# Attention and gated MLP on one core: the load of the next pair's values moved forward in the loop, partial outputs stored from SyncE, small products limited to 24 a pair

## The chip, the core and the metric

One core of one Trainium2 chip runs the whole program. The metric is device microseconds of one execution; the time before is the median of 3 runs. Engines have the profile's names: PE multiplies, PEld loads its weights, DVE, ACT and POOL do elementwise work, and SP only issues DMAs. An engine's queue runs in order: an instruction that waits holds all that stand behind it on the same engine.

## What is computed

Block-causal attention over 8 batches and 8 heads (576 positions of 64), then a gated MLP over the 4608 tokens of 512 features:

```python
scores = scale * np.matmul(q, k.transpose(0, 1, 3, 2))
scores = np.where(block_i >= block_j, scores, -1000000000.0)
attn = softmax(scores)                      # over the keys
x = (attn @ v).transpose(0, 2, 1, 3).reshape(B * S, H * D)
out = (1 / (1 + np.exp(-(x @ w_gate))) * (x @ w_val)) @ w_out
```

## The kernel before, in words

Two heads of one batch make a **pair**; there are 32, numbered p = 0 to 31, and four of them are a batch. The first stage goes through the pairs. While a pair's scores, softmax and value products run, PE's gaps are filled with products of the first third of the MLP (`mlp1`) for the batch before. The second stage, from about 660 us on, does the rest of the MLP with dense products (L1253, L1338).

Up to p = 7 the probabilities are transposed on PE. From p = 8 on (`rest`) DVE transposes them into `ZV` in blocks of 32, and the value products are 32x64 tiles, done in two runs of 144 rows each: `z_run` at the step `half` of the pair, and again at the step `AV`, which opens the next pair. The lists `JOIN` (p = 8) and `REST` (p = 9 to 31) give the order of a pair's steps, each with a number of places at which MLP products are dealt out; a pair of `REST` has 36. In `REST` the steps are: `AV` of the pair before, `s` and `t` (scores), `sl`, the transposes, `ml`, `half`, `r` (reciprocal sums to `r_d` and broadcast back as `rb`), `k`, `FX` (the pair before is finished: POOL multiplies `xT` by `rb` at L739, ACT cuts `XH` at L741, SP stores `xT_d` at L746), `q`, `v`.

The loads are SP's. Steps `k` and `q` load keys and queries of pair p+3 (L316, eight DMAs), step `v` loads the values of pair p+1 (L283, eight DMAs of 144 KB in runs of 256 bytes). Values of odd and even pairs have a buffer each: `VR` for even p, a part of the tile `ZV` for odd p. So a row `bank<-ZV,VR` is of an even pair and `bank<-ZV` alone of an odd one. A value load may start when the second run of the pair two before, which read the same buffer, is done. `behind` pins each value load behind the last query load (or `rb`) on SP, so SP's order is: r_d, k, rb, k, q, values, xT_d, and again r_d.

Each batch's `mlp1` ends with four copies out of PSUM by ACT (L866, into `ost`, two buffers), each stored to `part_d` (L869) by ACT's own DMA queue. All hardware DMAs, of whatever engine, share eight completion semaphores in turn, so a DMA also waits until the one eight before it in the program has landed; for the store this can be a value load that SP has still to issue.

`filling(p)` puts small products of one column (`bank<-ident`) in front of the first value run, so that PE's count of issued instructions, modulo 256, stands in `WINDOW` there. Each is two rows on PE.

Of the kernel before, what the change touches and what calls it, by code (L numbers as in the profile page):

```python
# [21 lines left out]
NX = 256  # L22
AHEAD = 3
KEEP = (52, 40)
WINDOW = (140, 152)

CONV_DUE = ([(0, 5), (0, 10), (1, 10), (2, 10), *((p, 9) for p in range(3, 7))], [(6, 1), (7, 2), (7, 8), (8, 1)])

# [1 line left out]
         ("tr3", 1), ("r", 0), ("ld", 0))  # L30
ALONE = (("S3", 1), ("TR2", 1), ("warm", 0), ("k", 1), ("S2", 1), ("q", 1), ("m3", 0), ("m2", 0), ("TRt", 1), ("t", 1), ("TRl", 1), ("sl", 1), ("AV", 2),
         ("tr3", 1), ("r", 0), ("FX", 0), ("ld", 0))
REST = (("AV", 0), ("s", 0), ("t", 9), ("sl", 3), ("tr3", 2), ("trt", 3), ("ml", 0), ("tr2", 0), ("trl", 0), ("half", 3),
        ("r", 3), ("k", 4), ("FX", 3), ("q", 3), ("v", 3))
JOIN = (("s", 0), ("t", 9), ("AV", 8), ("sl", 3), ("tr3", 2), ("trt", 3), ("ml", 0), ("tr2", 0), ("trl", 0), ("half", 2),
        ("r", 2), ("k", 2), ("q", 3), ("v", 2))
TURN = (("s3", 1), ("TR2", 1), ("k", 0), ("s2", 1), ("TRt", 1), ("q", 0), ("t", 1), ("TRl", 1), ("sl", 1), ("AV", 1),
        ("tr3", 1), ("r", 0), ("tr2", 1), ("trl", 1), ("trt", 3))
N_FIRST = 7
# [3 lines left out]
FETCH, FETCH_AT = 256, 192  # L43
# [6 lines left out]
def attn_glu_kernel(ctx: ExitStack, tc: tile.TileContext, q, k, v, w_gate, w_val, w_out, out):  # L50
    nc = tc.nc
# [3 lines left out]
    P = 128  # L55
# [8 lines left out]
    part_d = dram.tile([NTOK, DM], F32, name="part_d")  # L64
# [155 lines left out]
    with ExitStack() as s2:  # L220
# [55 lines left out]
        def load(p, what, queue=nc.sync):  # L276
            b, hp = pairs[p]
            h0 = 2 * hp
            if what == "v" and p > N_FIRST:
                VR = VRs[(p + 1) % 2]  # L280
                for a in range(4):
                    for h in range(2):
                        dma = nc.sync.dma_start(out=VR[32 * a:32 * a + 32, h],  # L283
                                                in_=v[b, h0 + h].rearrange("(t p) d -> p t d", p=32))
                        behind(dma.ins, last["SPq"])
                        last["SPq"] = dma.ins
                loads["SP"] = dma.ins
                return
            if what == "v":
                VS = VSs[p % 3]  # L290
                for h in range(2):
                    bulk(nc.sync.dma_start(out=VS[:, 0:4, h * D:(h + 1) * D],
                                           in_=v[b, h0 + h, 0:4 * P, :].rearrange("(t p) d -> p t d", p=P)))
                dma = nc.sync.dma_start(out=VS[64:128, 4, :].rearrange("p (h d) -> p h d", h=2),
                                        in_=v[b, h0:h0 + 2, 4 * P:S, :].rearrange("h p d -> p h d"))
                bulk(dma)
                loads["SP"] = dma.ins
                return
            if p <= NP:

                i, src = (0, k) if what == "k" else (1, q)
                r = rqks[p % 2].rearrange("p i s -> p (i s)").rearrange("p (t c) -> p t c", c=P)
                for h in range(2):
                    bulk(queue.dma_start(out=r[:, 4 * i:4 * i + 4, h * D:(h + 1) * D],
                                         in_=src[b, h0 + h, 0:4 * P, :].rearrange("(t p) d -> p t d", p=P)))
                dma = queue.dma_start(out=r[64 * i:64 * i + 64, 8, :].rearrange("p (h d) -> p h d", h=2),
                                      in_=src[b, h0:h0 + 2, 4 * P:S, :].rearrange("h p d -> p h d"))
                bulk(dma)
                if queue is nc.sync:
                    mark("SP", dma)  # L310
                return

            r, src = (rqks[p % 2][:, 0], k) if what == "k" else (rqks[p % 2][:, 1], q)
            for h in range(2):
                for j in range(2):
                    dma = bulk(queue.dma_start(  # L316
                        out=r[64 * h + 32 * j:64 * h + 32 * j + 32].rearrange("p (t a) -> p t a", a=32),
                        in_=src[b, h0 + h, :, 32 * j:32 * j + 32].rearrange("(t p) a -> p t a", p=32)))
                    if p > N_FIRST + 3:
                        last["SPq"] = dma.ins  # L320
# [5 lines left out]
        def filling(p):  # L326

            x = (FETCH_AT - issued[0] - WAITS[0] - WAITS[1] * p // 4) % FETCH
            lo, hi = WINDOW
            return 0 if lo <= x <= hi else -(-((x - hi) % FETCH) // 4)  # L330

        def mark(engine, ins):
            last[engine] = ins.ins
# [530 lines left out]
        def out_done(b, t, ps):  # L864
            ost = mp.tile([P, DM], F32, name="t" if b == B and t > 1 else "ost", bufs=2)
            nc.scalar.mul(out=ost, in_=ps, mul=0.5)  # L866
            if b < B:
                r = b * S + t * P
                nc.scalar.dma_start(out=part_d[r:r + P, :], in_=ost)  # L869
            else:  # L870
                for j in range(2):
                    r = (2 * t + j) * S + NM
                    nc.gpsimd.dma_start(out=part_d[r:r + 64, :], in_=ost[64 * j:64 * j + 64, :])
# [293 lines left out]
        for p in range(n + 1):  # L1167
            early_work(p, 0)
            pr = prep(p + 1) if p + 1 < n else iter(())
            now = attend(p) if p < n else None  # L1170
            tick = 0
            steps = (ALONE if p < NP else FIRST if p < N_FIRST else TURN if p == N_FIRST else
                     JOIN if p == N_FIRST + 1 else REST)
            ticks = sum(places for _, places in steps)
            lined[0] = line if N_FIRST < p < n else no_line
            for what, places in steps:
                if what.startswith(("AV", "TR", "FX")):
                    if prev:
                        prev(what.lower() if what in ("AV", "FX") else what.lower()[:2] + what[2:])
                    if prev and what == "AV" and pairs[p - 1][1] == NP - 1:  # L1180
                        pb = pairs[p - 1][0]
                        mlp = itertools.chain(mlp, mlp1(pb, mbank if p < n else bank))
                        left += F1 * 6 * NC + 3 * F1 * 4
                elif what in "kq":
                    next(pr, None)
                    if p >= N_FIRST and p + 3 < n:
                        load(p + 3, what)
                elif what == "v":
                    if p + 1 < n:
                        load(p + 1, "v")  # L1190
                elif what == "ld":
                    for x in "kq":
                        load(p + 3, x)
                elif now:
                    hot[0] = p > N_FIRST and (hot[0] or what == "s")
                    now(what)
                    if what == "trt" and p > N_FIRST:
                        hot[0] = False
                        settle()
                new = what == "AV" and pairs[p - 1][1] == NP - 1  # L1200
                if p <= N_FIRST and new and p:
                    rate = (left - KEEP[0]) / (4 * TICKS)
                elif p > N_FIRST and (new or what == steps[0][0]):
                    i = p % NP
                    rate = max(0, left - KEEP[1]) / (ticks - tick + (NP - 1 - i) * PLACES) if i or new else 1.0
                for _ in range(places if now else 6 if what == "AV" else 0):
                    pe_ticks.append(pe_last[0])
                    acc += rate
                    while acc >= 1:
                        acc -= 1  # L1210
                        left -= 1
                        issued[0] += 2
                        ins = next(mlp, None)
                        if ins is not None:
                            if dealt and p > N_FIRST:
                                behind(ins, dealt[0])
                            dealt[:] = [ins]
                            recent[:] = [*recent[-7:], ins]
                            if hold:
                                behind(ins, hold[0])  # L1220
                            ahead_by = 0 if p > N_FIRST + 1 and what == "t" or p != N_FIRST + 1 and what == "trt" else AHEAD
                            if len(pe_ticks) > ahead_by:
                                behind(ins, pe_ticks[-1 - ahead_by])
                    tick += 1
                    convert_to(p, tick)
                    early_work(p, tick)
            run(pr)
            if p == N_FIRST:
                load(p + 1, "v")
            if 0 < p and p + 2 <= N_FIRST:  # L1230
                load(p + 2, "v")
            prev = now
# [267 lines left out]
```

## Time and profile before

| | |
|---|---|
| median of 3 runs (lowest to highest) | 1266.76 us (1261.48 to 1269.65) |
| the profiled execution, its span | 1266.42 us, 1264.6 us |
| mean granted TensorE clock | 0.957 |
| pairs 9 to 28 (153.2 to 581.0) | 427.8 us |
| PE busy in them | 379.1 us |

A pair is counted from its first `bank<-KH,QH` product of 512 columns to that of the next pair; pair 20 begins at 390.2, pair 21 at 414.2, pair 22 at 431.3. In the windows view each row is one stretch: its length, then busy time and number of instructions of each engine (PE, PEld, DVE, ACT, POOL), then the granted clock of PE as a share of full speed, the DMA engines' busy share and GB/s. In a timeline a row gives start, length, engine, line, operation and tiles, the number of merged instructions, and in brackets the idle time before it and what ended it. SPq and ACTq rows are the issuing of DMAs, not their transfer.

### The profile page before, as it was taken

What the parts mean: (1) busy time and instruction counts of PE and PEld (TensorE: products, weight loads), DVE (VectorE), ACT (ScalarE), POOL (GpSimd) and SP (SyncE); (2) the same over time, 40 slices, a digit from 0 to 9 for tenths busy, and PEclk for the clock granted to TensorE, in tenths of its full rate; (3) what the DMA queues carried; (4) which work ended last, traced back from release to release, by engine and by line L of the source; (5) the groups of instructions that cost most, each with busy time, mean ns of one, the idle gap of its engine ahead of it and who ended that gap; (6) DMA issues with size and microseconds to landing.
All of it is one profiled execution on the core that took longest, in us unless ns stands there. A gap on an engine that the chain in (4) does not pass through costs nothing.

```text
span 1264.6 us, 32228 instructions
## 1 busy us (share of the span) xinstructions
PE 1186.0 (94%) x12851; PEld 947.3 (75%) x12851; DVE 888.2 (70%) x1748; ACT 573.7 (45%) x1370; POOL 340.4 (27%) x381
## 2 busy tenths in 40 slices
PE   8898889899898997999989999999999999999998
PEld 5565667677677775777768888888888888888888
DVE  5877645566556754675798695888999976768565
ACT  5866345455444543553524344354454432323222
POOL 3445313232133231323330110111111234142402
PEclk9999889889888987898999999999999999999999
DMA  7656565858676768586854114265387956253522
GB/s 162 171 140 143 110 132 99 154 101 127 126 136 126 142 107 165 98 134 129 161 146 136 67 51 134 47 187 158 69 217 246 319 174 209 87 179 108 167 95 89
DMA packets 396486, 175.42 MB, mean 139 GB/s; under 512 B 323248, under 2 KB 363184, under 8 KB 395696
## 3 DMA queue, kind: packets, MB, share of 16 engines
q1 hardware_dynamic: 388992, 161.92, 54.7%
q10 hardware_dynamic: 6960, 10.39, 2.5%
q8 instruction: 101, 1.65, 0.6%
q0 software_dynamic: 384, 1.05, 0.2%
q14 instruction: 49, 0.40, 0.1%
HBM read 125.96 MB, written 47.33 MB: 137 GB/s over the span
## 4 chain that ended last, share of the span: by engine, by line
PE 65%; DMA 8%; SPq 5%; DVE 5%; issue 1%; ACT 1%; ACTq 0%; DVEq 0%
PE b L1253 25%; PE bank L354 11%; PE m L160 11%; PE b L1338 7%; PE m L1338 7%; PE m L167 4%; DMA ZV<-in_v_dram 3%; DMA VR<-in_v_dram 2%; SPq L316 2%; PE bank L160 1%; SPq L283 1%; PE bank L167 1%; DMA r_d<-rT 1%; DVE XL L1069 1%; DMA xT_d<-xT 1%
## 5 line engine op out<-in xcount | busy, mean ns | idle before, releaser
L1253 PE MATMUL b<-XH,w 128*128 128x512 f32 (+1 forms) x1120 | 320.8, 368 | 1.0 <-ACT p L1271 0.9
L1253 PEld LDWEIGHTS b<-XH,w 128*128 128x128 f32 x1120 | 203.5, 188 | 37.5 <-ACT p L1271 1.3
L1253 PE MATMUL b<-XL,w 128*128 128x512 f32 (+1 forms) x560 | 205.6, 368 | 0.0
L498 ACT ACTIVATE P<-bank,nm 128x512 f32<-128x512 f32 (+3 forms) x256 | 131.9, 525 | 21.3 <-DVE nm L490 20.8
L490 DVE TENSOR_REDUCE nm<-bank 128x2 f32<-128x1024 f32 (+3 forms) x128 | 100.6, 816 | 31.5 <-ACT bank L531 29.7
L1253 PEld LDWEIGHTS b<-XL,w 128*128 128x128 f32 x560 | 105.5, 188 | 17.6
L1066 ACT CAST XH<-XB 128x1024 fp32r<-128x1024 f32 (+1 forms) x72 | 66.9, 943 | 89.4 <-DVE XB L1064 54.5
L535 DVE MEMSET bank<- 64x128 f32 x24 | 4.0, 165 | 137.0 <-PE bank L354 137.0
L354 PE MATMUL bank<-ZV,VR 32*64 32x80 f32 (+4 forms) x3456 | 72.6, 275 | 25.4 <-DMA VR<-in_v_dram 22.8
L167 PE MATMUL m<-wo,hH 128*128 128x512 f32 x256 | 93.0, 434 | 2.6 <-ACT ost L866 2.6
L1338 PE MATMUL m<-wo,hH 128*128 128x512 f32 x288 | 93.3, 389 | 0.0
L1338 PE MATMUL b<-wo,hH 128*128 128x512 f32 x288 | 92.9, 389 | 0.0
L656 DVE STREAM_TRANSPOSE ZV<-P 128x512 f32<-128x512 f32 (+1 forms) x192 | 87.5, 491 | 7.0 <-ACT P L498 5.9
L1051 POOL TENSOR_TENSOR XB<-XB 128x256 f32<-128x256 f32 x30 | 24.6, 820 | 246.3 <-DMA XB<-xT_d 191.6
L354 PEld LDWEIGHTS bank<-ZV,VR 32*64 32x64 f32 x3456 | 60.4, 152 | 37.1 <-DMA VR<-in_v_dram 30.4
L1069 DVE TENSOR_TENSOR XL<-XB,XH 128x1024 fp32r<-128x1024 f32 (+1 forms) x72 | 78.2, 1091 | 13.6 <-ACT XH L1066 13.4
L160 PE MATMUL m<-XH,wg 128*128 128x512 f32 x240 | 86.7, 421 | 0.0
L160 PE MATMUL m<-XH,wv 128*128 128x512 f32 x240 | 84.7, 411 | 0.9 <-DVE h L205 0.9
L354 PE MATMUL bank<-ZV 32*64 32x48 f32 (+5 forms) x3680 | 77.5, 260 | 3.2 <-DMA ZV<-in_v_dram 3.0
L354 PEld LDWEIGHTS bank<-ZV 32*64 32x64 f32 (+1 forms) x3680 | 61.8, 132 | 18.7 <-issue 4.6
L739 POOL TENSOR_TENSOR xT<-xT,rb 128x576 f32<-128x576 f32 x24 | 34.6, 1440 | 131.9 <-ACT xT L714 83.7
L167 PEld LDWEIGHTS m<-wo,hH 128*128 128x128 f32 x256 | 53.1, 213 | 16.5 <-ACT ost L866 5.2
(214 smaller groups left out, 2493.7 us busy)
## 6 DMA issues: line engine op xcount, KB each, us to landing
VR<-in_v_dram SPq DMA_DIRECT2D x96, 144.0 KB
ZV<-in_v_dram SPq DMA_DIRECT2D x96, 144.0 KB
XB<-xT_d SPq DMA_DIRECT2D x48, 256.0 KB
prr<-part_d SPq DMA_DIRECT2D x46, 256.0 KB
part_d<-ost SPq DMA_DIRECT2D x36, 256.0 KB
part_d<-ost ACTq DMA_DIRECT2D x32, 256.0 KB
xT_d<-xT SPq DMA_DIRECT2D x28, 288.0 KB
rqk<-in_k_dram SPq DMA_DIRECT2D x108, 72.0 KB
```

The costliest lines, as they stand in the source:

```text
L160: mm = nc.tensor.matmul(ps, lhsT=lh, rhs=rh, start=(i == 0), stop=(i == n - 1))
L167: mm = nc.tensor.matmul(ps, lhsT=lh[:, f, t * P:(t + 1) * P], rhs=rh, start=(f == i == 0), stop=(f == F1 - 1 and i == 2))
L316: dma = bulk(queue.dma_start(out=r[64 * h + 32 * j:64 * h + 32 * j + 32].rearrange("p (t a) -> p t a", a=32), in_=src[b, h0 + h, :, 32 * j ...
L354: pe_last[:] = [nc.tensor.matmul(*args, **kw).ins]
L490: line("DVE", nc.vector.tensor_reduce(out=nm[:, c0:c0 + 2], in_=ps[:, :, c:c + P * (i + 1)], axis=AX.X, op=ALU.max, negate=True), rest)
L498: line("ACT", nc.scalar.activation(out=Pi[:, h], in_=ps[:, h, c:c + n], func=AF.Exp, bias=nm[:, c0 + h:c0 + h + 1], accum_out=sm[:, 5 * h ...
L656: line("DVE", nc.vector.transpose(out=dst[:, :, :4 * ZG].rearrange("p b (g x) -> p b g x", g=4)[:, :, :i + 1, :32], in_=Pi[:, h].rearrange ...
L739: nc.gpsimd.tensor_mul(out=xT, in0=xT, in1=rb)
L1066: cut = nc.scalar.copy(out=XO[j][0][:, a:b, c], in_=x)
L1069: sub = nc.vector.tensor_sub(out=XO[j][1][:, a:b, c], in0=x, in1=XO[j][0][:, a:b, c].bitcast(F32))
L1253: mm = nc.tensor.matmul(ps, lhsT=lh, rhs=rh, start=(first and k == 0), stop=(k == n - 1), skip_group_check=not first)
L1338: mm = nc.tensor.matmul(po[t], lhsT=lh[:, f, t * P:(t + 1) * P], rhs=rh, start=(half == 0 and i == 0), stop=(half == 1 and i == 5))
```

## The change

Three edits. The step `v` stands behind `t` in `REST` (9 places after the scores) and behind `AV` in `JOIN`; its places went to `q`, so no other step moves; for p = 7 the load of pair 8's values moves from the pair's end to behind `sl`. The 32 stores of `part_d` are issued by SP instead of ACT. `filling` gives at most 24.

```diff
-WINDOW = (140, 152)
+WINDOW, MOST = (140, 152), 24
-REST = (("AV", 0), ("s", 0), ("t", 9), ("sl", 3), ("tr3", 2), ("trt", 3), ("ml", 0), ("tr2", 0), ("trl", 0), ("half", 3),
-        ("r", 3), ("k", 4), ("FX", 3), ("q", 3), ("v", 3))
-JOIN = (("s", 0), ("t", 9), ("AV", 8), ("sl", 3), ("tr3", 2), ("trt", 3), ("ml", 0), ("tr2", 0), ("trl", 0), ("half", 2),
-        ("r", 2), ("k", 2), ("q", 3), ("v", 2))
+REST = (("AV", 0), ("s", 0), ("t", 9), ("v", 0), ("sl", 3), ("tr3", 2), ("trt", 3), ("ml", 0), ("tr2", 0), ("trl", 0), ("half", 3),
+        ("r", 3), ("k", 4), ("FX", 3), ("q", 6))
+JOIN = (("s", 0), ("t", 9), ("AV", 8), ("v", 0), ("sl", 3), ("tr3", 2), ("trt", 3), ("ml", 0), ("tr2", 0), ("trl", 0), ("half", 2),
+        ("r", 2), ("k", 2), ("q", 5))
-            return 0 if lo <= x <= hi else -(-((x - hi) % FETCH) // 4)
+            return 0 if lo <= x <= hi else min(-(-((x - hi) % FETCH) // 4), MOST)
-                nc.scalar.dma_start(out=part_d[r:r + P, :], in_=ost)
+                nc.sync.dma_start(out=part_d[r:r + P, :], in_=ost)
+                    if what == "sl" and p == N_FIRST:
+                        load(p + 1, "v")
-            if p == N_FIRST:
-                load(p + 1, "v")
```

What it moves on SP, between the query loads of pair 8's step `q` and the `rb` loads of pair 9. Before:

```order
L316 DMA rqk_93<-in_k_dram 32x18x32 x2
L316 DMA rqk_93<-in_q_dram 32x18x32 x4
L283 DMA ZV<-in_v_dram 32x18x64 x8
L746 DMA xT_d<-xT 128x576
L588 DMA r_d<-rT 9x32 x4
L316 DMA rqk_92<-in_k_dram 32x18x32 x2
L593 DMA rb<-r_d 64x512
```

The same place of the changed kernel:

```order
L316 DMA rqk_93<-in_k_dram 32x18x32 x2
L316 DMA rqk_93<-in_q_dram 32x18x32 x4
L869 DMA part_d<-ost 128x512
L283 DMA VR_95<-in_v_dram 32x18x64 x8
L746 DMA xT_d<-xT 128x576
L869 DMA part_d<-ost 128x512 x2
L588 DMA r_d<-rT 9x32 x4
L316 DMA rqk_92<-in_k_dram 32x18x32 x2
L593 DMA rb<-r_d 64x512
```

The value load keeps its place between q and xT_d, but it is now that of pair 10 (`VR`), where it was that of pair 9 (`ZV`): one pair earlier. Stores of `ost` stand before and behind it.

On ACT, in the pair in which a batch's first three copies to `ost` come (pair 12; pairs 16, 20 and so on are alike). Before:

```order
L869 DMA part_d<-ost 128x512 x2
L430 CAST KH<-KQ 128x576
L431 ACTIVATE QH<-KQ 128x448
L741 CAST XH_428<-xT 128x512
L866 ACTIVATE ost<-m 128x512
L869 DMA part_d<-ost 128x512
L714 COPY xT<-bank_2935 128x2x4x32
```

Now:

```order
L430 CAST KH<-KQ 128x576
L431 ACTIVATE QH<-KQ 128x448
L741 CAST XH_428<-xT 128x512
L866 ACTIVATE ost<-m 128x512
L714 COPY xT<-bank_2943 128x2x4x32
```

The stores are gone from in front of the copies to `xT` (L714), which free the PSUM banks that the next pair's scores need; nothing else on ACT moves. On PE only the small products change: 52, 16, 12 and 11 of them in pairs 8 to 11 become 24, 24, 24 and 19, and the 20 pairs after those keep their 14 or 15. DVE and POOL have the same order as before.

## Rows read from the trace of the kernel before

**Rows 1.** Page, busy time of the engines, share of the span, instructions.

```profile
PE 1186.0 (94%) x12851; PEld 947.3 (75%) x12851; DVE 888.2 (70%) x1748; ACT 573.7 (45%) x1370; POOL 340.4 (27%) x381
```

**Rows 2.** Windows: pairs 13, 19, 20, 22 and 23, and the sum of pairs 9 to 28.

```profile
241.40:265.40 24.00, 18.26 (x386) 14.48 (x384) 12.45 (x27) 9.82 (x30) 5.17 (x6) 0.86 0.64 120
...
373.80:390.20 16.40, 16.37 (x389) 13.17 (x384) 13.65 (x28) 9.89 (x30) 6.85 (x7) 1.00 0.61 109
390.20:414.20 24.00, 20.74 (x385) 16.01 (x382) 11.56 (x26) 9.82 (x30) 5.36 (x10) 0.86 0.76 151
...
431.30:455.10 23.80, 20.83 (x386) 16.25 (x382) 12.04 (x27) 10.09 (x30) 6.65 (x11) 0.86 0.79 136
455.10:471.30 16.20, 16.20 (x390) 13.06 (x382) 12.60 (x28) 9.83 (x30) 6.62 (x7) 1.00 0.65 100
...
sum 427.80, PE 379.06 PEld 298.66 DVE 247.52 ACT 199.19 POOL 120.84; mean PE 18.95 PEld 14.93 DVE 12.38 ACT 9.96 POOL 6.04
```

**Rows 3.** Windows: a stretch inside pair 20.

```profile
402.50:409.30 6.80, 6.18 (x140) 5.17 (x141) 0.97 (x2) 0.69 (x2) 2.98 (x6) 0.50 0.43 115
```

**Rows 4.** Waits of PE and ACT, whole run: us in total, times, longest.

```profile
PE bank L354 <- DMA VR<-in_v_dram: 22.8, 44, 1.2
PE bank L354 <- ACT xT L714: 22.7, 7, 5.7
...
ACT xT L714 <- DMA ZV<-in_v_dram: 26.4, 4, 8.2
```

**Rows 5.** Timeline of PE, pair 20, around its first value run.

```profile
398.11 0.43 PE L354 MATMUL bank<-ident 32*64 32x1 f32 x30
...
403.56 2.34 PE L354 MATMUL bank<-ZV,VR 32*64 32x48 f32 x130 [0.49 <-DMA VR<-in_v_dram]
```

**Rows 6.** Timeline of SP's queue: value loads and what follows them, four places.

```profile
287.22 6.16 SPq L283 DMA_DIRECT2D ZV<-in_v_dram  x8
293.48 1.87 SPq L746 DMA_DIRECT2D xT_d<-xT  x1
...
307.57 5.93 SPq L283 DMA_DIRECT2D VR<-in_v_dram  x8
...
393.62 5.96 SPq L283 DMA_DIRECT2D VR<-in_v_dram  x8
...
400.63 2.23 SPq L588 DMA_DIRECT2D r_d<-rT  x4
...
411.97 5.68 SPq L283 DMA_DIRECT2D ZV<-in_v_dram  x8
...
474.83 5.62 SPq L283 DMA_DIRECT2D VR<-in_v_dram  x8
...
494.17 6.05 SPq L283 DMA_DIRECT2D ZV<-in_v_dram  x8
...
520.32 5.62 SPq L283 DMA_DIRECT2D VR<-in_v_dram  x8
...
538.07 5.83 SPq L283 DMA_DIRECT2D ZV<-in_v_dram  x8
```

**Rows 7.** Timeline of ACT: a copy and its store (pairs 12, 13), and pair 20.

```profile
238.78 0.60 ACT L866 ACTIVATE ost<-m 128x512 f32<-128x512 f32 x1 [1.10 <-PE m L167]
247.13 0.33 ACTq L869 DMA_DIRECT2D part_d<-ost  x1
...
402.59 0.60 ACT L741 CAST XH<-xT 128x512 fp32r<-128x512 f32 x1
```

**Rows 8.** Timeline of POOL, pair 22: the product with rb.

```profile
434.31 1.44 POOL L739 TENSOR_TENSOR xT<-xT,rb 128x576 f32<-128x576 f32 x1 [2.32 <-DMA rb<-r_d]
```

**Rows 9.** Timeline of PE, pair 8, first value run.

```profile
144.57 1.40 PE L354 MATMUL bank<-ZV,VR 32*64 32x48 f32 x66 [1.83 <-issue]
```

**Rows 10.** Timeline of SP's queue behind the last pair.

```profile
659.02 2.08 SPq L961 DMA_DIRECT2D raw<-in_moe_w_gate_dram  x4
```

**Rows 11.** Instructions on the tensor part_d; SP's own stores of the second stage: ns min/median/max.

```profile
L1353 SPq DMA_DIRECT2D part_d<-ost x36: 320/411/1752, 766.0 to 995.9; - x36
```

## The prediction

> **What bounds the kernel now.** The page comes first. PE is busy 1186 of 1264.6 us [rows 1]; it sets the end, and a change counts only if it takes idle time or slow time from PE. The second stage has none to give, so I cut the first stage into pairs with the windows view. Pairs 9 to 28, all steady `REST` pairs, take 427.8 us, 21.4 each [rows 2]. But a pair that nothing disturbs takes 16.2 or 16.4 us with PE busy throughout at clock 1.00, and others take 24 at clock 0.86 [rows 2]. At 16.4 the twenty would take 328 us: some 100 us stand in the disturbed ones.
>
> The waits view says what disturbs them. PE waits 22.8 us in 44 pieces for `VR` and 22.7 us in seven for ACT's copy of `xT` [rows 4]. Each wait is paid twice: behind pair 20's broken value run the clock stands at 0.50 for 6.8 us [rows 3], which is 1.2 of 2.4 GHz.
>
> The timelines show how each arises. **Values late.** Pair 20's first value run is ready at 398.1, but its load is issued by SP from 393.62 for 5.96 us, and PE gets the last of it at 403.56 [rows 5, 6]: about 10 us from first issue to the last landing. SP could not be earlier, because the load stands behind r_d, k, rb, k and q. So there is a loop: the run of pair p+1 waits for its values, these for SP's lap, and the lap starts with r_d of pair p, whose sums come just when pair p's run does. It explains the alternation of 16 and 24: a pair that was stretched gives SP time, and the next finds its values there. **ACT held.** In pair 13 ACT has finished the copy to `ost` at 239.4, but its store goes out only at 247.13 [rows 7], while the copies of `xT` stand behind it; ACT's idle time there, up to 8.2 us and 26.4 in all, ends with a value load [rows 4], the one whose semaphore the store shares. This makes pair 13 24.0 us long.
>
> **The change, part by part.** *Values one pair earlier.* They keep SP's place behind q and before xT_d, so they still go out near the start of a pair; but they are needed in the middle of the next one, some 16 us later than now. 10 us of landing fit into that. The new wait is for the second run that last read the buffer; it ends where the pair begins, in pair 20 at 390.2, and SP comes to its load at 393.62 [rows 2, 6], so I cost it at nothing; an SP that came early would wait there, and r_d behind it too. The 22.8 us of waits and their slow stretches go, as far as SP keeps up.
>
> *Stores on SP.* ACT no longer stands before a store, so the 22.7 us go too. SP gets 32 more issues, on average one a pair. ACT issues one in 0.33 us, SP its own stores of the second stage in 0.41 median, 1.75 at most [rows 7, 11]. Where a store stands in front of r_d it partly fills time in which SP waits for the values to land anyway: I take 0.25 a pair, bounds 0 and 0.41.
>
> For this part a rule of the Trainium skill can be set against a row. ACT's store row lasts 0.33 us and starts 7.7 us after its copy ended [rows 7]. The page "DMA: Bandwidth & Descriptors", section "Issuing engines are not separate DMA queues", says that starting DMAs from several engines saves only the time the sequencer needs to initiate them, usually small. By it the move gives 32 x 0.33 = 10.6 us of ACT's time and leaves PE's wait on `xT`, 22.7 us: the sum below would come to 1231. The row contradicts this: what the store costs ACT is the wait in front of it. I go by the row.
>
> *What limits the pairs then.* With both waits gone PE could do a pair in 16.4 us, and SP's lap becomes the question. I read it from one value load to the next. Where r_d followed xT_d at once, a lap took 411.97 - 393.62 = 18.35 us, and 494.17 - 474.83 = 19.34; where SP rested a little before r_d, 538.07 - 520.32 = 17.75 [rows 6]. In none of these did SP wait long for PE. r_d right behind the values takes 2.23 us for its four issues [rows 6], because the values must land first. None of this changes, so SP is slower than PE: the next thing late is SP's `rb`, its stores, and at last the values again. I take 18.35 + 0.25 = 18.6 us a pair: 20 x 18.6 = 372.0, against 427.8 a gain of 55.8. Bounds: 17.75 with stores free (72.8), and 19.34 + 0.41 = 19.75 (32.8).
>
> *PE's lead.* PE may run ahead of SP until one of SP's products is missing. `rb` has about 8 us: POOL's product with it starts 3.0 us into pair 22 and takes 1.44 [rows 2, 8], and ACT's cut of its result comes 12.4 us into pair 20 [rows 2, 7]. A store of `ost` may have next to nothing, since the third copy of a batch reuses the first one's buffer. At the end, where no more keys and values are loaded, SP catches up, so the lead is kept: 4 us gained, bounds 0 and 8.
>
> *Small products.* 91 in pairs 8 to 11 before, 91 after: the same PE time. They move PE's place in its instruction stream, which the row of pair 8 prices: a value run broken for 1.83 us by "issue" [rows 9]. That stall can go (-1.8), or appear in pairs 8, 9 and 10 (+5.5 if all three are new). I take +1.
>
> *Stores behind the last pair.* There SP's weight loads leave in groups, one at 659.02 that takes 2.08 us [rows 10], and the third stores of batches 6 and 7 each stand behind such a group. ACT's copies have two buffers: I take +1, bounds 0 and 3.
>
> Sum against the profiled execution's own 1266.4 us (0.3 below the median of the runs): 1266.4 - 55.8 - 4 + 1 + 1 = 1208.6, so **1209 us**. With all bounds good 1266.4 - 72.8 - 8 - 1.8 = 1184, with all bad 1266.4 - 32.8 + 5.5 + 3 = 1242.
>
> **The rivals.** *PE sets the pace (0.10).* SP's laps could shrink when no run is late. Then 20 x 16.4 = 328: 1266.4 - 99.8 = 1167. Against it: no lap read here is under 17.75.
>
> *The stores cost SP what xT_d sometimes does (0.13).* xT_d behind the values took 1.87 us at 293.48, and that lap 307.57 - 287.22 = 20.35 [rows 6]; SP also rested in it, so it is a high price. Twenty such make 407: 1266.4 - 20.8 = 1246. A rule speaks for this: the Trainium skill, same page, "Queues, rings and completion order", says that on each DMA engine one queue's descriptors are taken in ring order while the engine takes turns between queues; a store from SP therefore stands behind the values' descriptors, where ACT's took turns with them. No run here shows such a store yet.
>
> *Nothing is gained (0.08).* If laps with stores take 21.4, or PE's waits only change their names, it stays at 1266, within 1% (1254 to 1279).
>
> *Slower (0.06).* The place is ACT's copy to `ost`: two buffers, a store that now stands behind eight value loads, and the copies of `xT` behind it on ACT. Each time it holds ACT as in pair 13, the pair costs 24.0 instead of 16.4. Two of a batch's four pairs hit give 20.2 a pair, still a gain; from three on the mean is 22.1, 0.7 over the 21.4 of now, and with four 24.0: 1281 to 1319, I say 1300. Against it: only the third copy of a batch follows its buffer's store closely.
>
> **The numbers.** The SP-paced case has 0.63 (1184 to 1242). About 1% is what a measurement of this kernel can tell from no change. Faster by more: 0.63 + 0.10 + 0.12 of the store case = 0.85; within 1%: 0.09; slower: 0.06. For 8 in 10 the range takes the SP-paced case, the store case up to 1250, and the near edge of the PE-paced one: 1172 to 1250.
>
> **What would show it.** Right: no PE wait on `VR` worth naming, none of ACT on a value load, SP issuing without rest from pair 9 to 28 at 18 to 19 us from value load to value load, pairs of about that length, and fewer slow stretches. Wrong in the lap: pairs of 16.4 with SP resting before r_d, or laps over 20 with long stores. Wrong in the stores: ACT's copies to `ost` waiting for `part_d`. Wrong in the small products: "issue" gaps of 1 to 3 us in value runs of pairs 8 to 10.

## The result and the profile after

The changed kernel takes 1212.4 us (median of 4 runs, 1211.4 to 1215.8) where the kernel before, on the same chip, takes 1268.2: a ratio of 0.957 (95% interval 0.952 to 0.962). The forecast was 1209, with a range of 1172 to 1250. The profiled execution has a span of 1209.6 us against 1264.6, 55.0 less, and a mean granted clock of 0.979 against 0.957.

Page of the kernel after, busy time of the engines, which answers to [rows 1]:

```profile
PE 1148.2 (95%) x12851; PEld 921.4 (76%) x12851; DVE 891.5 (74%) x1748; ACT 572.6 (47%) x1370; POOL 339.2 (28%) x381
```

PE issues the same 12851 products and is busy 37.8 us less: with less of the time at the low clock the same products are shorter.

Windows view of the kernel after, with the columns of [rows 2]: pairs 9, 10, 11, then 20 to 23, then the sum of pairs 9 to 28.

```profile
155.60:175.80 20.20, 18.12 (x411) 14.59 (x409) 11.56 (x26) 10.42 (x31) 4.75 (x7) 1.00 0.82 157
175.80:199.10 23.30, 20.23 (x411) 16.23 (x409) 12.67 (x28) 10.48 (x31) 6.88 (x9) 0.85 0.71 119
199.10:217.50 18.40, 17.98 (x401) 14.52 (x399) 12.51 (x28) 9.79 (x30) 7.00 (x9) 1.00 0.74 120
...
353.20:370.50 17.30, 16.75 (x390) 13.17 (x384) 12.70 (x26) 9.34 (x29) 6.64 (x11) 1.00 0.82 137
370.50:397.00 26.50, 18.91 (x387) 15.00 (x384) 13.53 (x27) 10.49 (x31) 5.49 (x6) 0.81 0.92 172
397.00:414.30 17.30, 16.56 (x385) 13.26 (x382) 12.04 (x27) 9.98 (x30) 6.62 (x11) 1.00 0.77 134
414.30:430.50 16.20, 16.20 (x390) 13.08 (x382) 12.87 (x28) 9.78 (x30) 6.31 (x7) 1.00 0.79 130
...
sum 366.10, PE 340.89 PEld 272.34 DVE 248.83 ACT 198.04 POOL 120.47; mean PE 17.04 PEld 13.62 DVE 12.44 ACT 9.90 POOL 6.02
```

The alternation of 16 and 24 is gone. Most pairs take 16 to 18 us at clock 1.00. Two kinds still stand out: pairs 9 and 10, where the limited small products are, and every fourth pair (21 here with 26.5 us; 25 and 29 take 22.7 and 23.2, 17 only 18.5). Pairs 9 to 28 lost 61.7 us, but pair 9 begins 2.4 us later than before, and pairs 29 and 30 (23.2 and 18.9 us) together take 6.6 us more. Behind them 2.3 us are gained.

Waits view of the kernel after, PE and then ACT (us in total, times, longest), which answers to [rows 4]:

```profile
PE bank L354 <- ACT xT L714: 19.8, 4, 7.6
PE bank L354 <- issue: 12.5, 5, 3.5
...
ACT ost L866 <- DMA part_d<-ost: 37.0, 5, 10.6
```

"Issue" is idle time in which PE waited for nothing that the profile shows. No wait of PE on `VR` is left, and none of ACT on a value load. PE's wait for the copy of `xT` has kept its size and changed its cause: it now comes four times, each behind a copy to `ost` that waits for a store.

How that happens is seen in the timelines of the kernel after around pair 21: SP's queue, then ACT, then PE (start, length, engine, line, operation, tiles, count, idle time in front and what ended it).

```profile
364.53 2.21 SPq L316 DMA_DIRECT2D rqk<-in_q_dram  x2
366.85 6.08 SPq L283 DMA_DIRECT2D ZV<-in_v_dram  x8
373.02 0.92 SPq L746 DMA_DIRECT2D xT_d<-xT  x1
374.04 0.88 SPq L869 DMA_DIRECT2D part_d<-ost  x2
375.01 1.80 SPq L588 DMA_DIRECT2D r_d<-rT  x4
```
```profile
360.57 1.06 ACT L866 ACTIVATE ost<-m 128x512 f32<-128x512 f32 x2
...
378.02 0.60 ACT L866 ACTIVATE ost<-m 128x512 f32<-128x512 f32 x1 [10.60 <-DMA part_d<-ost]
378.51 0.82 ACT L714 COPY xT<-bank 128x256 f32<-128x256 f32 x4
```
```profile
379.02 0.69 PE L354 MATMUL bank<-KH,QH 64*128 64x384 f32 x2 [7.59 <-ACT xT L714]
```

The batch's first two copies are ready at 361.6. Their stores leave at 374.0, behind keys, queries, values and xT_d. The third copy needs the first one's buffer, so ACT stands from 367.4 to 378.0 with the copies to `xT` behind it, and PE waits 7.6 us. The slow clock comes with it:

Windows view of the kernel after, the stretch around that wait:

```profile
374.50:384.70 10.20, 5.68 (x19) 4.66 (x20) 3.53 (x8) 4.38 (x13) 0.00 (x0) 0.50 0.57 145
```

The clock stands at 1.2 of 2.4 GHz for 10.2 us, and pair 21 takes 26.5 us, where pair 23 takes 16.2.

### The profile page after: what moved, and what is told of

Same layout as the page of the kernel before. It is cut to its first block, busy times and chain, and to the rows that moved or that the text cites. A ratio compares the mean times of both kernels' runs of the same rounds, so it can differ in the third digit from the quotient of the medians.

```text
span 1209.6 us, 32242 instructions
## 1 busy us (share of the span) xinstructions
PE 1148.2 (95%) x12851; PEld 921.4 (76%) x12851; DVE 891.5 (74%) x1748; ACT 572.6 (47%) x1370; POOL 339.2 (28%) x381
## 4 chain that ended last, share of the span: by engine, by line
PE 73%; DVE 11%; DMA 5%; issue 4%; ACT 4%; POOL 2%; SPq 1%; DVEq 0%; ACTq 0%; POOLq 0%
PE b L1253 26%; PE bank L354 13%; PE m L160 11%; PE b L1338 7%; PE m L1338 7%; PE m L167 5%; DVE nm L490 2%; ACT P L498 2%; PE bank L160 1%; DMA part_d<-ost 1%; DMA r_d<-rT 1%; PE bank L167 1%; DVE XL L1069 1%; DMA rb<-r_d 1%; DVE ZV L656 1%
## 5 line engine op out<-in xcount | busy, mean ns | idle before, releaser
L1253 PEld LDWEIGHTS b<-XL,w 128*128 128x128 f32 x560 | 105.6, 188 | 17.9 <-DVE XL L1069 0.3
L1338 PE MATMUL m<-wo,hH 128*128 128x512 f32 x288 | 93.2, 389 | 0.0
L167 PE MATMUL m<-wo,hH 128*128 128x512 f32 x256 | 86.7, 407 | 1.7 <-ACT ost L866 1.7
L354 PE MATMUL bank<-ZV 32*64 32x48 f32 (+5 forms) x3680 | 75.0, 258 | 2.7 <-issue 2.5
L354 PE MATMUL bank<-ZV,VR 32*64 32x80 f32 (+4 forms) x3456 | 53.7, 253 | 10.2 <-issue 6.5
L1338 PEld LDWEIGHTS b<-wo,hH 128*128 128x128 f32 x288 | 54.1, 188 | 11.2
```

Source lines behind the costliest of these rows:

```text
L167: mm = nc.tensor.matmul(ps, lhsT=lh[:, f, t * P:(t + 1) * P], rhs=rh, start=(f == i == 0), stop=(f == F1 - 1 and i == 2))
L354: pe_last[:] = [nc.tensor.matmul(*args, **kw).ins]
L1253: mm = nc.tensor.matmul(ps, lhsT=lh, rhs=rh, start=(first and k == 0), stop=(k == n - 1), skip_group_check=not first)
L1338: mm = nc.tensor.matmul(po[t], lhsT=lh[:, f, t * P:(t + 1) * P], rhs=rh, start=(half == 0 and i == 0), stop=(half == 1 and i == 5))
```

## The experiments

My theory was: SP's lap sets the pace of pairs 9 to 30. The two waits removed are worth little unless SP's lap is short; PE's other waits, the one on `ost` included, are where PE stands while SP catches up. The main rival: the `ost` wait itself is what the changed kernel loses time to. The table gives every kernel's median, its ratio to the kernel before with the interval, and from the windows view the 22 pairs 9 to 30, a pair on average, and the clock in them. The kernel before was measured again beside them, at 1268.3 us for the first four experiments, 1264.4 for the next four and 1265.8 for the last two, so kernels of different groups are compared by the ratios first.

| kernel | us | ratio (95%) | pairs 9 to 30 | a pair | clock |
|---|---|---|---|---|---|
| before | 1268.2 | 1 | 463.3 | 21.1 | 0.90 |
| after | 1212.4 | 0.957 (0.952-0.962) | 408.2 | 18.6 | 0.96 |
| values alone | 1218.6 | 0.960 (0.955-0.966) | 411.1 | 18.7 | 0.95 |
| stores alone | 1242.5 | 0.981 (0.974-0.988) | 439.4 | 20.0 | 0.93 |
| after, no limit | 1203.8 | 0.948 (0.943-0.953) | 398.1 | 18.1 | 0.97 |
| after, third buffer | 1212.8 | 0.956 (0.951-0.961) | 401.6 | 18.3 | 0.97 |
| after, four more issues | 1241.0 | 0.981 (0.977-0.984) | 435.6 | 19.8 | 0.93 |
| after, q loads on POOL | 1192.3 | 0.942 (0.937-0.947) | 387.7 | 17.6 | 0.99 |
| no limit, no products in pair 8 | 1203.0 | 0.951 (0.948-0.954) | 405.3 | 18.4 | 0.96 |
| no limit, stores on POOL | 1198.4 | 0.949 (0.945-0.953) | 392.2 | 17.8 | 0.97 |
| no limit, q loads on POOL | 1186.5 | 0.938 (0.936-0.941) | 381.3 | 17.3 | 1.00 |
| the same, no products in pair 8 | 1179.8 | 0.933 (0.930-0.935) | 384.2 | 17.5 | 0.99 |

**Values alone** (the changed kernel with the other two edits undone):

```diff
-            return 0 if lo <= x <= hi else min(-(-((x - hi) % FETCH) // 4), MOST)
+            return 0 if lo <= x <= hi else -(-((x - hi) % FETCH) // 4)
-                nc.sync.dma_start(out=part_d[r:r + P, :], in_=ost)
+                nc.scalar.dma_start(out=part_d[r:r + P, :], in_=ost)
```

> The kernel before with the value loads moved alone: the stores stay on ACT, small products without a limit. Theory (two causes, values late and ACT held): PE's 22.8 us of waits on VR go, ACT is still held before its stores and PE still waits some 20 us for the copies of xT, each with a slow stretch; time 1215 to 1245. Rival (the values alone are the gain, ACT's waits would only have moved): about 1205, as the changed kernel without its issue gaps.

1218.6 us. The move of the values alone takes most of the gain. Waits view of this kernel, ACT and then PE:

```profile
ACT xT L714 <- DMA rb<-r_d: 33.5, 5, 7.2
...
PE bank L354 <- ACT xT L714: 28.1, 5, 6.7
```

ACT is held before its stores as it was before; only the load that shares the semaphore is now `rb`, no longer the values. (The trace numbers the semaphores: the store that leaves ACT at 303.17 in this run has number 105, and so has the `rb` load that SP issued at 300.17.)

**Stores alone** (the kernel before with the 32 stores on SP):

```diff
-                nc.scalar.dma_start(out=part_d[r:r + P, :], in_=ost)
+                nc.sync.dma_start(out=part_d[r:r + P, :], in_=ost)
```

> The kernel before with the 32 stores on SP alone: values are still requested at the pair's end, small products without a limit. Theory: PE's wait on ACT's copies of xT falls by most of its 22.7 us, but the loop run, r_d, SP's lap, values, run stays and now holds the stores too: pairs of 20.3 to 20.6 on average, 20 x 20.5 = 410 against 427.8, so about 1249 (1240 to 1262), and PE's waits on VR grow over 22.8 us. Rival (the stores alone are the gain): 1205 to 1215.

1242.5 us, 26 less than before. Waits view of PE in this kernel:

```profile
PE bank L354 <- DMA VR<-in_v_dram: 19.6, 40, 0.9
PE bank L354 <- DMA ZV<-in_v_dram: 8.2, 21, 0.8
```

PE's wait on the copy of `xT`, 22.7 us in [rows 4], has no row any more; the wait on the values stays, 27.8 us. So the two edits remove two separate waits, and each is worth something without the other. Together (without the limit) they gain 64.5 us, less than 49.7 + 25.8 = 75.5: the pace that is left is shared.

**After without the limit:**

```diff
-            return 0 if lo <= x <= hi else min(-(-((x - hi) % FETCH) // 4), MOST)
+            return 0 if lo <= x <= hi else -(-((x - hi) % FETCH) // 4)
```

> The changed kernel without the limit of 24 (52, 16, 12 and 11 small products in pairs 8 to 11 as before). Theory: the limit cost time, since PE's waits on issue in pairs 8 to 10 rose from 1.8 to 8.7 us and a slow stretch of 6.8 us came with them; without it the time falls by 4 to 9 us, to 1203 to 1208. Rival (SP paces these pairs too, so issue gaps lie in its shadow): 1211 to 1213.

1203.8 us. The intervals of the two ratios just overlap, so the medians' 8.6 us is a rough size, but the profile puts it in one place. Windows view of this kernel, pairs 9, 10, 11, with the same columns as above:

```profile
152.60:170.30 17.70, 17.70 (x396) 14.35 (x391) 11.56 (x26) 10.32 (x31) 4.76 (x7) 1.00 0.86 168
170.30:188.00 17.70, 17.70 (x391) 14.32 (x385) 12.71 (x28) 10.49 (x31) 7.32 (x9) 1.00 0.72 147
188.00:205.60 17.60, 17.60 (x384) 14.28 (x381) 12.52 (x28) 9.78 (x30) 7.00 (x9) 1.00 0.82 138
```

The three take 53.0 us with PE never idle, and 61.9 with the limit. Pair 8 is 27.2 us here and 27.3 there, and pairs 12 to 30 take 345.1 and 346.3. The limit costs 8.9 us in pairs 9 to 11, where value runs are broken by "issue" (2.1 us in pair 9, 3.1 in pair 10) and the clock falls in pair 10. The profiled spans differ by 12.4 us, but 2.9 of these lie ahead of pair 8, where the two kernels are the same.

**After with a third buffer for `ost`** (a buffer of the same size that is free then):

```diff
-            ost = mp.tile([P, DM], F32, name="t" if b == B and t > 1 else "ost", bufs=2)
+            ost = mp.tile([P, DM], F32, name="t" if b == B and t > 1 else "h2" if b < B and t == 2 else "ost", bufs=2)
```

> The changed kernel with a third buffer for the copies to ost (the third copy of a batch takes a buffer of h2, which is idle then), so that it need not wait for the first one's store. Theory (SP's lap is the pace, ost is only where PE's lead ends): ACT's 37 us of waits on part_d and PE's 19.8 us on xT go, but PE then runs into the next product of SP that is late, rb; value load to value load stays 18.6 and the time falls by the larger lead alone, 3 to 9 us, to 1203 to 1209. Rival (the two buffers of ost are themselves the pace): all of the 19.8 us and half of the slow stretches behind them go, pairs fall to 16.5 to 17, time 1180 to 1190.

1212.8 us: nothing gained, where I expected some. ACT's wait on the stores fell from 37.0 to 9.7 us, PE's waits on `xT` are gone, and pair 31 begins at 556.7 instead of 563.8. But the end came no earlier. SP's queue says why: the last value load and what follows it, in the kernel after and then with the third buffer.

```profile
548.91 5.78 SPq L283 DMA_DIRECT2D ZV<-in_v_dram  x8
555.48 1.77 SPq L961 DMA_DIRECT2D raw<-in_moe_w_gate_dram  x1
557.35 1.41 SPq L588 DMA_DIRECT2D r_d<-rT  x4
```
```profile
551.40 5.21 SPq L283 DMA_DIRECT2D ZV<-in_v_dram  x8
557.40 1.78 SPq L961 DMA_DIRECT2D raw<-in_moe_w_gate_dram  x1
559.27 1.58 SPq L588 DMA_DIRECT2D r_d<-rT  x4
```

SP gets there no earlier, even 2 us later. PE then waits under other names, 3.5 us for `h` in pair 31 (1.0 in the kernel after) and, behind that pair, 4.7 us for `XH` (3.0), which stands behind `rb`. So the `ost` wait is where PE stood, not what paced it: the rival falls.

**After with four more issues a pair on SP** (copies of 9x32 in front of r_d, which nobody reads):

```diff
+                if rest:
+                    spare = dram.tile([9, P], F32, name="spare", bufs=2)
+                    for j in range(4):
+                        nc.sync.dma_start(out=spare[:, 32 * j:32 * j + 32], in_=rT[32 * j:32 * j + 9])
```

> The changed kernel with four more DMAs a pair on SP, copies of the four small stores of r_d into a place that nothing reads (1.1 KB each). Theory (SP's lap sets the pair): the lap grows by four issues of about 0.33 us, 1.3 to 1.5 us, and PE follows: 20 to 22 pairs x 1.4 = 28 to 31 us more, 1235 to 1248. Rival (PE or the volume of the transfers sets the pair, SP has slack): under 5 us more, 1212 to 1217.

1241.0 us. Timeline of SP's queue in this kernel:

```profile
388.00 1.75 SPq L590 DMA_DIRECT2D spare<-rT  x4
```

The four cost SP 1.75 us here (1.4 to 2.1 in other pairs), and a pair becomes 1.25 us longer (19.80 against 18.55); over 22 pairs that is 27.4 of the 28.6 us lost by the medians (30 by the ratios). PE, ACT, DVE and POOL have the same work as in the kernel after.

**After with the q loads of pairs 11 to 31 issued by POOL:**

```diff
+            queue = nc.gpsimd if what == "q" and p > N_FIRST + 3 else queue
-                    if p > N_FIRST + 3:
+                    if p > N_FIRST + 3 and queue is nc.sync:
```

> The changed kernel with the query loads of the later pairs (from pair 11 on, four DMAs a pair) issued by POOL instead of SP. Theory (SP's lap is serial: values, xT_d, r_d, k, rb, k, q): it loses the 2.06 us of q and falls from 18.6 to about 16.5, PE's own pace; pairs 13 to 28 from 18.1 to 16.5 to 17, 15 to 25 us less, 1187 to 1197, if POOL issues them in time. Rival (the DMA engines' volume is the pace, whoever issues): laps stay at 18 to 19, 1208 to 1215.

1192.3 us, 20 less than the changed kernel. SP's queue in this kernel, one lap:

```profile
373.22 5.97 SPq L283 DMA_DIRECT2D VR<-in_v_dram  x8
379.29 0.70 SPq L747 DMA_DIRECT2D xT_d<-xT  x1
...
389.49 6.01 SPq L283 DMA_DIRECT2D ZV<-in_v_dram  x8
395.59 0.68 SPq L747 DMA_DIRECT2D xT_d<-xT  x1
399.82 1.37 SPq L589 DMA_DIRECT2D r_d<-rT  x4
```

This lap takes 16.27 us, and SP now rests 3.5 us before r_d; the 17 laps from 216.0 to 512.2 take 17.4 on average. How long SP stood before r_d until the sums in `rT` were ready, over the whole run, in the kernel before, the kernel after and this one:

```profile
SPq L588 <- DVE rT L585: 121.7, 26, 10.2
```
```profile
SPq L588 <- DVE rT L585: 24.6, 8, 5.1
```
```profile
SPq L589 <- DVE rT L586: 67.8, 26, 5.7
```

In the kernel after, SP waits so only 8 times, and in no pair from 13 to 30: there it is SP that is late. With the q loads on POOL it waits again in every pair from 9 to 30, 0.8 to 5.8 us. Waits view of this kernel, ACT and PE:

```profile
ACT ost L867 <- DMA part_d<-ost: 3.3, 1, 3.3
...
PE bank L355 <- POOL QBL L441: 7.2, 8, 1.1
```

The `ost` wait shrank from 37.0 to 3.3 us without a buffer being added, and PE's waits on `xT` went with it. PE now paces most pairs (busy 370.3 of the 387.7 us of pairs 9 to 30, at clock 0.99); what it still waits for is small and comes from POOL, which has the q loads now.

**No limit, and no small products in pair 8** (4, 12 and 11 in pairs 9 to 11):

```diff
+            if p == N_FIRST + 1:
+                return 0
```

> The changed kernel without the limit and without any small product in pair 8 (0, 4, 12, 11 in pairs 8 to 11, the rest as before). Theory (52 small products in front of a value run drain PE's instructions and cause pair 8's issue gap of 3.6 us themselves): the gap goes and 1.2 us of small products too, 3 to 5 us less than without the limit alone: 1199 to 1201. Rival (the gap is from the place alone): it stays, 1202 to 1205.

1203.0 us, which the ratios can't tell from the run without the limit. Pair 8 became 5.6 us shorter (21.6 us at clock 1.00) and pair 9 3.6 longer; the rest was given back in SP-paced pairs. Inconclusive by itself, it is taken up below.

**No limit, and the stores on POOL's queue:**

```diff
-                nc.sync.dma_start(out=part_d[r:r + P, :], in_=ost)
+                nc.gpsimd.dma_start(out=part_d[r:r + P, :], in_=ost)
```

> The changed kernel without the limit, with the stores of the partial outputs issued by POOL instead of SP. Theory: SP's lap loses the 0.4 us of stores, and a store no longer stands behind eight value loads, so ACT's waits on part_d (37 us) and PE's 18 us on xT go; PE then stands before SP's next late product (rb), as with a third buffer: 1196 to 1203. Rival (a store elsewhere than on SP holds its engine, as it held ACT): POOL held, 1205 to 1220.

1198.4 us. A pair is 0.27 us shorter in the profile (17.83 against 18.10), but the ratios are equal (0.949 and 0.948): stores cost SP little. The rival's 1205 to 1220 did not come, and ACT's wait for the stores, 37.0 us in the kernel after, is 13.0.

**No limit, and the q loads on POOL,** then **the same without small products in pair 8** (edits as shown above):

> Changed kernel with both single edits together: no limit on the small products, and the q loads of pairs 11 to 31 issued by POOL. Theory (SP's lap paced the pairs, and the limit takes away PE time in pairs 9 to 11 only): with q on POOL the pairs are paced by PE, so what the limit costs in pairs 9 to 11 (60.1 us with it and q on POOL, 53.0 without it) is gained in full: 1192.3 - 7 = 1185 us, 1181 to 1189. Rival (SP or POOL still paces the later pairs, and a lead gained early is given back as in the run with the third ost buffer): 1190 to 1194.

1186.5 us, 5.8 less than with the limit; the intervals overlap, but in the profile pairs 9 to 30 are 6.4 us shorter, 6.6 of it in pairs 9 to 11 (53.5 against 60.1).

> As the run before it (no limit, q loads on POOL), and no small products in pair 8 (then 4, 12 and 11 in pairs 9 to 11). In the run with SP's q loads this made pair 8 shorter by 5.6 us and pair 9 longer by 3.6, and nothing was kept. Theory (SP took back what PE gained): with SP out of the way the difference is kept: 2 us under the run before it, 1180 to 1186. Rival (an issue gap comes at another place): the same as the run before it or up to 3 above.

1179.8 us, 6.7 less, and more than I expected. This is the fastest version: 0.933 of the kernel before, and 32.6 us under the changed one by the medians. Not all of the 6.7 can be put down to the edit: of the 5.7 us by which the profiled spans differ, 3.3 lie ahead of pair 8, where the two kernels are the same. Timelines of PE in pair 8, with 104 products of one column and with none:

```profile
142.44 1.18 PE L355 MATMUL bank<-ident 32*64 32x1 f32 x104 [0.57 <-ACT P L499]
143.45 1.05 PE L355 MATMUL bank<-ZV,VR 32*64 32x48 f32 x78
148.11 1.40 PE L355 MATMUL bank<-ZV,VR 32*64 32x48 f32 x66 [3.60 <-issue]
```
```profile
139.45 2.23 PE L357 MATMUL bank<-ZV,VR 32*64 32x48 f32 x144
144.78 0.61 PE L357 MATMUL bank<-ZV,VR 32*64 32x80 f32 x25
145.81 2.06 PE L357 MATMUL bank<-ZV,VR 32*64 32x144 f32 x119 [0.41 <-issue]
150.62 0.44 PE L357 MATMUL bank<-KH,QL 64*128 64x384 f32 x1 [1.52 <-issue]
```

With none, the first value run goes through in one piece, and the gaps that remain are 0.41 us, and 1.52 at the start of pair 9. Pair 8 takes 22.3 us at clock 1.00 instead of 28.0 at 0.88. Behind the 1.52 us gap pair 9 takes 21.1 instead of 17.8, so pairs 8 to 11 together are 2.7 us shorter (78.8 against 81.5), near the 2 that were expected. Since SP no longer paces the pairs, these are kept: pairs 12 to 30 take 327.7 us with none and 327.8 with the 104.

## Why the prediction was right, point by point

*Both waits go.* Half right. The wait on `VR` is gone, and without the values' move it stays; ACT no longer stands before a store, and without the stores' move it does. But "the 22.7 us go too" is wrong: PE's wait on the copy of `xT` is still 19.8 us, now because ACT's copies to `ost` wait for SP's stores, which the prediction had listed as the sign of being wrong in the stores. It did not spoil the sum, since SP's lap was the pace with or without it, as the third-buffer run shows.

*SP's lap then paces the pairs, 18.35 + 0.25 = 18.6 us.* Right in mechanism and size. From 218.59 to 534.43 SP issues 18 value loads, a lap of 315.84 / 17 = 18.58 us, and the 22 pairs take 18.55 each. "SP issuing without rest from pair 9" holds from pair 13 on; in pairs 9 to 12, three of which the small products stretched, SP still rested 1.2 to 5.1 us before r_d. The run with four more issues and the one with the q loads on POOL move the time both ways. The rival in which PE sets the pace at 16.4 needs SP out of the way: that run comes to 17.6, of which PE is busy 16.8, so even PE alone needs more than 16.4.

*Stores at 0.25 a pair, and the rival that they cost what xT_d sometimes does.* Of the 32 stores in SP's queue 28 took 0.32 to 0.48 us and four 0.9 to 1.7, and with POOL issuing them a pair was 0.27 us shorter. The rival's 1246 is wrong: its 1.87 us came for a few stores, not for one in each pair. The rule beside it, from the Trainium skill's page "DMA: Bandwidth & Descriptors", section "Queues, rings and completion order", is not tested by this, since no row shows in what order descriptors were taken; what the rival drew from it for the time did not come. The rule of the Trainium skill, same page, section "Issuing engines are not separate DMA queues", by which the sum was 1231, is answered by the stores-alone run: it gained 26 us and removed PE's wait on `xT`, where 0.33 us of issue time for each store would have left it.

*PE's lead, 4 us gained.* Wrong in its last step: "At the end, where no more keys and values are loaded, SP catches up, so the lead is kept". Pairs 9 to 28 were 61.7 us shorter, 5.9 more than the lap's 55.8, but pairs 29 and 30 gave 6.6 back. The third-buffer run shows that this was not the `ost` wait's doing: with it gone PE came 7.1 us earlier to pair 31, and the end still came 1.9 us later. A lead over the pacing engine is not a gain where the last work needs that engine too.

*The `ost` wait* stood in the rival on the slower side, with "only the third copy of a batch follows its buffer's store closely" against it. Both halves held: it came once a batch, up to 10.6 us, and so the pairs stayed far under the 21.4 at which it would have decided.

*Small products, +1.* Mis-sized: "91 before, 91 after: the same PE time" was right, but the stall was priced by one gap of 1.83 us and no slow clock. "Issue" gaps in pairs 8 to 10 came to 8.7 us, and pairs 9 to 11 took 8.9 us more than without the limit, past my bound of 5.5. The forecast still came within 4 us: of the 61.9 us of pairs 9 to 11 the lap had already counted 3 x 18.6 = 55.8, and pairs 12 to 28, at 17.9, ran ahead of it.

Put together in the span: -55.8 for the lap, +6.1 for pairs 9 to 11 over it, -12.0 for pairs 12 to 28 under it, +6.6 in pairs 29 and 30, +2.4 ahead of pair 9 and -2.3 behind pair 30 make -55.0. The forecast had -57.8. Its small terms were off by more than their sum shows: +5.1 for the small products, -1.4 for the lead (-5.4 where -4 was forecast), -3.3 behind the last pair, and +2.4 ahead of pair 9 for which it had no term. That these cancel to 2.8 us is luck; the lap is not. Nor is the +2.4 shown to come from the change: PE has an "issue" gap at 104 to 107 us, ahead of everything in which the kernels with the values' move differ from each other, and in them it took 1.5 to 3.7 us, and pair 8 began at 124.6 to 128.8.

*Stores behind the last pair, +1.* Not seen: behind pair 30 the span is 2.3 us shorter than before, past the good bound of 0. Why was not tried.

What stays open: why the value runs break where they do, and why the gap at 104 to 107 us differs between kernels that are the same up to there. That the small products move the gaps, and that none in pair 8 removes the largest, was measured; the rule of `WINDOW` by which they were placed was not tested.

## What to carry to other kernels

When a wait is taken away, add up one whole turn of the queue that issues the loads, waits for landings included: here that number, 18.6 us, gave the new time better than any wait on the compute engines. Then give the pacing queue less to issue (four loads on another queue were worth 20 us) before adding buffers where a compute engine happens to stand (a third one was worth nothing here). And look at filler work again after each change, for in pairs 8 to 11 it was worth 3 to 9 us to have it in the right pair or not at all.

## What the runs showed of the hardware that I had not expected

- A few small DMAs are dear on a queue that paces: four copies of 9x32 took SP 1.4 to 2.1 us a pair, and the kernel took some 30 us more.
- An engine that issues a store can be held by somebody else's load: ACT stood in front of stores of 0.33 us for up to 8.2 us behind value loads, and, with the values moved, up to 7.2 us behind `rb`.
- Products of one column can cost more than their time, by where they stand: with 48 (24, two rows each) in each of pairs 8, 9 and 10 the value runs were broken for 3.5, 2.1 and 3.1 us; with 104, 32 and 24 for 3.6 us in pair 8 and not in the next two; and with none in pair 8 for 0.4 us, and its clock stayed at 1.00 where it was 0.87 to 0.88.
